# Chunked attention and a maxout layer by seven products: two operands split later, the output products in another order

## The chip, the cores and the metric

The kernel runs on one core of a Trainium2 chip. The metric is the device time of one execution in microseconds (us), given as the median of several runs. Its engines are TensorE (PE in the profile; PEld is its weight load), VectorE (DVE), ScalarE (ACT), GpSimd (POOL) and SyncE (SP), which issues the transfers (DMAs). Each runs its own instructions in the order in which the program lists them and waits where an operand, a bank or a buffer is not ready.

## What is computed

```python
scores = scale * np.matmul(q_c, k_c.transpose(0, 1, 2, 4, 3))    # 576 tokens in chunks of 64
scores = scores - np.max(scores, axis=-1, keepdims=True)
attn = np.exp(scores)
attn = attn / (np.sum(attn, axis=-1, keepdims=True) + 1e-09)
out = np.matmul(attn, v_c)
...
h = np.maximum(np.maximum(x @ w1, x @ w2), x @ w3)               # x: 4608 x 512, w: 512 x 768
return (h @ w_out).astype(np.float32)                            # w_out: 768 x 512
```

Batch 8, 8 heads, head size 64; the attention output of all heads, 4608 tokens of 512 values, goes through a layer that keeps the largest of three products, and then through an output layer. All in float32.

## The kernel before

A float32 matrix product is done as three products of a reduced type: each operand is split into a high part (a cast) and a low part (what the cast lost), and low x high, high x low and high x high are added up in one bank of PSUM. ACT does the casts (`high`), DVE the subtractions (`low`).

The tokens come in tiles of 128. The first 8 tiles (two groups of 4) go through both layers directly, and while they do, the weights are mixed for the rest: the other 28 tiles, in four units of 7, 8, 7 and 6 tiles (`UNITS`), are computed by Strassen's scheme in Winograd's form. It takes seven products of blocks instead of eight; the operands of the products are sums and differences of blocks. Half a unit is 448, 512, 448 or 384 columns wide.

One unit has a hidden phase and an output phase. The hidden phase has nine sets (`sets`: three parts jp of the hidden width, for each of the three weights w). A set is seven products in the order `ORDER` = 1, 6, 5, 2, 7, 3, 4, each of 6 matmuls (L567). Products 2, 7 and 3 add onto the banks of 1, 6 and 5 (`banks_of_product`), once ACT has copied those out (`kept`, L581); five banks are taken in turn. Behind them DVE and POOL form the sums (L584, L587, L591) and the maximum over the three weights (L578). Behind every third set the operands of the output phase are made from the maximum: differences (L609, L621), casts (L614) and lows (L617), called Y. The output phase multiplies the seven Y operands with the mixed output weights, in the order `OUTER`: 18 matmuls a product, in two halves m of 9. Its products are read out by copies (L655, L666) and by DVE's sums (L658), which write the results to one of four output buffers (`ao`) that are stored by SP (L650).

The operands of the next unit's hidden phase, X1 to X7, are made during the output phase of the unit before (`operands`, L500 to L504): differences of blocks of the attention output in `stage` (L489, three by DVE or POOL), casts (L494) and lows (L498). The attention of the next units runs in between, a tile at a time: V, S and T are its products and transposes on PE (L258, L223, L246), `softmax` its steps on the others, and `tiles(u, time)` says when each tile of a unit is due. The output layer's weights are mixed once, by `store_out`: POOL adds (L419, L433), ACT's cast (L438), DVE's low (L441) and stores; `stores_out` plans it into unit 0's first sets. Mixed weights come back from DRAM a piece at a time, issued by SP (L510 for the hidden layer, L518 for the output layer), each into a ring whose previous content has been used.

What sets the order of all this is a list of due times. Every PE step advances a clock `now` by a nominal duration, and what a product leads to is planned at an offset from its end:

```python
    def passed(step):
        nonlocal now
        now += step
        while due and due[0][0] <= now:
            _, _, pe, fn = heapq.heappop(due)
            fn()
```

So the numbers in `operands`, in `after[...]` of `hidden` and in `tiles` and `stores_out` order the instructions on each engine; they are no times of the chip.

Of the kernel before, what the change touches and what calls it, by code (L numbers as in the profile page):

```python
# [31 lines left out]
OUTER = (1, 2, 6, 7, 5, 3, 4)  # L32
SOFTMAX = (("mx", 1.0), ("sub", 1.9), ("exp", 2.8), ("sum", 3.8), ("eps", 4.7), ("rec", 4.9), ("nrm", 5.3))
ON_PE = {"V": 0.6, "S": 0.6, "T": 0.35}
OPERANDS = 0.3
# [28 lines left out]
def chunk_attn_maxout_kernel(  # L64
# [399 lines left out]
    def unit(t0, count, rooms):  # L464
# [35 lines left out]
        def operands():  # L500
            return [(0.0, high(1)), (1.2, low(1)), (2.4, mix(5, b12, b11, nc.vector)), (3.4, high(5)),
                    (3.6, mix(6, b22, source[5], nc.vector)), (4.6, mix(7, b22, b12, nc.gpsimd)), (4.8, high(6)),
                    (5.8, low(6)), (5.9, high(2)), (7.0, low(5)), (8.0, mix(4, b21, source[6], nc.gpsimd)), (8.2, low(2)),
                    (8.3, high(7)), (9.4, low(7)), (9.45, high(3)), (10.6, low(3)), (10.7, high(4)), (11.8, low(4))]  # L504
# [10 lines left out]
        def load_outer(k):  # L515
            def fn():
                outer[k] = next_ring((k + 1) % 2, 6).rearrange("p (j k) x -> p j (k x)", j=3)
                nc.sync.dma_start(out=outer[k].bitcast(F32), in_=outer_w["w"].rearrange(  # L518
                    "p (j i x) -> p j i x", j=3, i=7)[:, :, k])
            return fn  # L520
# [49 lines left out]
        def hidden(n, loads):  # L570
# [3 lines left out]
            def M(k, c):  # L574
                return m()[:, k, c, :half]
# [26 lines left out]
            if w == 2:  # L602
# [17 lines left out]
                def less(eng, out, x, y):  # L620
# [4 lines left out]
                             (1.0, less(nc.gpsimd, t[7], lambda: M(1, 1), lambda: M(0, 1))), (1.6, t6), (1.65, high(2)),  # L625
                             (2.4, low(2)), (2.4, high(6)), (3.1, low(6)),
                             (3.2, less(nc.gpsimd, t[4], lambda: M(1, 0), t[6])), (3.1, high(5)), (3.8, low(5)),
                             (3.8, high(7)), (4.5, low(7)), (4.9, high(3)), (5.6, low(3)), (5.7, high(4)), (6.4, low(4))]
# [52 lines left out]
        return dict(operands=operands, load=load, load_outer=load_outer, hidden=hidden,  # L681
# [151 lines left out]
    def tiles(u, time):  # L833
        if u >= len(units):
            return
        lead = 14.0 if u == 1 else 18.0
# [45 lines left out]

    def stores_out():
        for jp in range(3):
            for at, fn in store_out(jp):
                plan(now + 16.0 + 14.0 * jp + at, 0.0, fn)
# [10 lines left out]
    parts += [("do", change), ("do", lambda: operands(0, OPERANDS)),  # L897
# [3 lines left out]
    for u, (it, t0, count) in enumerate(units):  # L901
# [4 lines left out]
        parts.append(("steps", lambda u=u, it=it: it["project"](loads_within(u))))  # L906
    now = -10.0
# [54 lines left out]
```

## Time and profile before

| | us |
|---|---|
| median of 3 runs | 642.67 (641.45 to 643.28) |
| the profiled execution | 643.57 |
| its span in the trace | 641.8 |

The profile is one execution. "Busy" is the time in which an engine executes; a bracket behind a row is the engine's idle time just before it and what it waited for last. PEclk is the clock that TensorE was granted, as a share of 2.4 GHz. Times are counted from the start of the span.

### The profile page before, as it was taken

To read this page: it belongs to the slowest core of one execution; us is meant where nothing else is said; L and a number is where in the kernel's file an instruction comes from. 1 tells how busy PE (TensorE), PEld (TensorE's weight loads), DVE (VectorE), ACT (ScalarE), POOL (GpSimd) and SP (SyncE) were. 2 spreads that over 40 slices of the span, in tenths; PEclk is the share of its full clock that TensorE was granted. 3 is DMA by queue.
4 is the path that set the end of the run, shared out by engine and by line. 5 is a ranking of instruction groups with operands and counts; after the bars stand their busy time and mean duration, and the time that the engine had idled before them with its cause. 6 is when DMAs were issued, how large, how long until landed. Compare 5 with 4: busy or idle time off the path is not lost.

```text
span 641.8 us, 12694 instructions
## 1 busy us (share of the span) xinstructions
PE 620.8 (97%) x5102; PEld 536.4 (84%) x5102; DVE 445.0 (69%) x684; ACT 269.9 (42%) x483; POOL 277.5 (43%) x235
## 2 busy tenths in 40 slices
PE   7899999999999899998999999989999998999997
PEld 3888878878888789997888888768989888999997
DVE  4889855788856958688368686883477568265762
ACT  4888633444543434362325252622342444232340
POOL 2423577764556824452234343441253434133430
PEclk9999999999999899998999999989999999999999
DMA  8978559666969996586866664759765657877774
GB/s 323 365 291 287 198 182 370 209 223 247 357 198 359 347 323 205 198 275 214 313 215 229 215 225 153 246 183 332 260 198 190 231 166 234 339 260 261 235 225 169
DMA packets 54219, 161.26 MB, mean 251 GB/s; under 512 B 4880, under 2 KB 17168, under 8 KB 49168
## 3 DMA queue, kind: packets, MB, share of 16 engines
q1 hardware_dynamic: 54160, 160.45, 72.2%
q8 instruction: 40, 0.66, 0.4%
q14 instruction: 19, 0.16, 0.1%
HBM read 128.97 MB, written 31.46 MB: 250 GB/s over the span
## 4 chain that ended last, share of the span: by engine, by line
PE 71%; DVE 17%; ACT 5%; issue 4%; POOL 2%; DMA 1%; SPq 0%; ACTq 0%; DVEq 0%; POOLq 0%
PE pm L567 53%; PE pm L173 4%; PE pm L174 4%; PE pm L175 4%; DVE X L498 3%; PE s L258 2%; PE tp L246 2%; DVE most L578 2%; PE s L223 2%; DVE e L233 2%; DVE mx L228 1%; DVE s L384 1%; DVE sm L181 1%; ACT e L237 1%; ACT stage L272 1%
## 5 line engine op out<-in xcount | busy, mean ns | idle before, releaser
L567 PE MATMUL pm<-X,ring 128*128 128x448 f32 (+2 forms) x1512 | 313.3, 367 | 4.4 <-ACT kept L581 3.3
L567 PEld LDWEIGHTS pm<-X,ring 128*128 128x128 f32 x1512 | 278.2, 189 | 32.4 <-ACT kept L581 5.1
L581 ACT COPY kept<-pm 128x448 f32<-128x448 f32 (+2 forms) x108 | 56.8, 532 | 149.9 <-PE pm L567 129.6
L567 PE MATMUL pm<-Y,ring 128*128 128x448 f32 (+2 forms) x504 | 107.7, 373 | 7.7 <-DVE ao L658 7.4
L567 PEld LDWEIGHTS pm<-Y,ring 128*128 128x128 f32 x504 | 94.4, 193 | 19.9 <-DVE ao L658 9.0
L591 POOL TENSOR_TENSOR kept<-kept 128x448 f32<-128x448 f32 (+2 forms) x36 | 43.5, 1209 | 82.5 <-ACT kept L581 82.3
L578 DVE TENSOR_TENSOR most<-pm,most 128x448 f32<-128x448 f32 (+2 forms) x72 | 44.6, 620 | 46.4 <-PE pm L567 45.0
L173 PE MATMUL pm<-xh,wl 128*128 128x512 f32 (+1 forms) x156 | 60.9, 391 | 0.0
L174 PE MATMUL pm<-xl,wh 128*128 128x512 f32 (+1 forms) x156 | 58.4, 375 | 0.3 <-DVE xl L269 0.3
L175 PE MATMUL pm<-xh,wh 128*128 128x512 f32 (+1 forms) x156 | 58.5, 375 | 0.0
L614 ACT CAST Y<-most 128x448 fp32r<-128x448 f32 (+2 forms) x72 | 39.6, 571 | 44.4 <-DVE most L578 44.4
L617 DVE TENSOR_TENSOR Y<-most,Y 128x448 fp32r<-128x448 f32 (+2 forms) x72 | 53.8, 777 | 3.0 <-ACT Y L614 1.6
L190 POOL TENSOR_TENSOR e<-e,sm 128x512 f32<-128x512 f32 x26 | 27.7, 1066 | 60.5 <-DVE sm L187 52.2
L587 POOL TENSOR_TENSOR kept<-kept 128x448 f32<-128x448 f32 (+2 forms) x24 | 30.5, 1269 | 52.0 <-DVE kept L584 43.2
L228 DVE TENSOR_REDUCE mx<-s 128x8 f32<-128x512 f32 x36 | 24.6, 683 | 27.3 <-PE s L223 27.3
L584 DVE TENSOR_TENSOR kept<-pm,kept 128x448 f32<-128x448 f32 (+2 forms) x36 | 22.3, 619 | 25.4 <-PE pm L567 21.8
L233 DVE TENSOR_TENSOR e<-s,mx 128x512 f32<-128x512 f32 x36 | 24.8, 690 | 18.3 <-ACT stage L272 17.6
L237 ACT ACTIVATE e<-e 128x512 f32<-128x512 f32 x36 | 22.7, 632 | 27.7 <-DVE e L233 27.7
L251 ACT COPY xs<-tp 128x512 f32<-128x512 f32 x36 | 21.0, 583 | 31.6 <-PE tp L246 31.6
L173 PEld LDWEIGHTS pm<-xh,wl 128*128 128x128 f32 x156 | 29.4, 188 | 5.4
L175 PEld LDWEIGHTS pm<-xh,wh 128*128 128x128 f32 x156 | 29.4, 188 | 5.4
L584 DVE TENSOR_TENSOR pm<-pm,kept 128x448 f32<-128x448 f32 (+2 forms) x48 | 30.0, 626 | 5.5 <-PE pm L567 4.3
(98 smaller groups left out, 855.6 us busy)
## 6 DMA issues: line engine op xcount, KB each, us to landing
ring<-w SPq DMA_DIRECT2D x36, 1024.0 KB, 5.2
ring<-w SPq DMA_DIRECT2D x36, 768.0 KB, 4.7
ring<-wo SPq DMA_DIRECT2D x28, 768.0 KB, 4.6
buf<-in_qk SPq DMA_DIRECT2D x36, 512.0 KB, 5.9
buf<-in_vb SPq DMA_DIRECT2D x36, 256.0 KB, 5.0
w<-s SPq DMA_DIRECT2D x18, 512.0 KB, 4.4
stage<-in_w SPq DMA_DIRECT2D x7, 512.0 KB, 4.6
out_t<-ao SPq DMA_DIRECT2D x16, 224.0 KB, 4.9
```

Of the source, the lines that this page charges most:

```text
L173: nc.tensor.matmul(out=o, lhsT=al, rhs=bh, start=first, stop=False)
L174: nc.tensor.matmul(out=o, lhsT=ah, rhs=bl, start=False, stop=False)
L175: nc.tensor.matmul(out=o, lhsT=ah, rhs=bh, start=False, stop=last)
L228: nc.vector.tensor_reduce(out=st["mx"].rearrange("p (g c) -> p c g", c=2), in_=st["s"], axis=AX.X, op=ALU.max)
L233: nc.vector.tensor_tensor(out=st["e"].rearrange("p g c k -> p c g k"), in0=st["s"], in1=most.unsqueeze(3).broadcast_to([P, 2, 4, 64]), op= ...
L567: nc.tensor.matmul(out=o[i], lhsT=a, rhs=b, start=new and k == 0, stop=last and k == 2, skip_group_check=i in banks_of_product)
L578: return lambda: nc.vector.tensor_tensor(out=M(k, c), in0=of(), in1=M(k, c), op=most)
L581: return lambda: nc.scalar.copy(out=kept(k), in_=o[i])
L584: return lambda: nc.vector.tensor_tensor(out=out(), in0=o[i], in1=kept(k), op=plus)
L591: (0.95, lambda: nc.gpsimd.tensor_tensor(out=kept(2), in0=kept(2), in1=kept(0), op=plus))],
L614: return lambda: nc.scalar.copy(out=y_room(i, jp)[:, 0, :half], in_=t[i]())
L617: return lambda: nc.vector.tensor_tensor(out=y_room(i, jp)[:, 1, :half], in0=t[i](), in1=y_room(i, jp)[:, 0, :half].bitcast(F32), op=minus)
```

## The change

Four things are changed. First, X3 and X4 leave `operands`; a new list, `last_operands`, makes their casts and lows at the start of the unit that uses them (for unit 0, behind the direct group's projection). Second, in `OUTER` product 4 now stands ahead of product 3, and the transfers of the output weights follow (`load_outer`). Third, the Y operands' casts and lows get other due times: Y5's cast first, Y4 ahead of Y3, and more time between them. Fourth, `store_out` begins 6 nominal us later and its three parts are 17 instead of 14 apart; the tiles of units 2 and 3 begin 2 later.

```diff
-OUTER = (1, 2, 6, 7, 5, 3, 4)
+OUTER = (1, 2, 6, 7, 5, 4, 3)
...
         def operands():
...
-                    (8.3, high(7)), (9.4, low(7)), (9.45, high(3)), (10.6, low(3)), (10.7, high(4)), (11.8, low(4))]
+                    (8.3, high(7)), (9.4, low(7))]
+
+        def last_operands():
+            return [(0.0, high(3)), (1.0, low(3)), (1.1, high(4)), (2.2, low(4))]
...
                 nc.sync.dma_start(out=outer[k].bitcast(F32), in_=outer_w["w"].rearrange(
-                    "p (j i x) -> p j i x", j=3, i=7)[:, :, k])
+                    "p (j i x) -> p j i x", j=3, i=7)[:, :, (0, 1, 2, 3, 4, 6, 5)[k]])
...
                 after[4] += [(0.2, less(nc.vector, t[5], lambda: M(0, 1), lambda: M(0, 0))),
-                             (1.0, less(nc.gpsimd, t[7], lambda: M(1, 1), lambda: M(0, 1))), (1.6, t6), (1.65, high(2)),
-                             (2.4, low(2)), (2.4, high(6)), (3.1, low(6)),
-                             (3.2, less(nc.gpsimd, t[4], lambda: M(1, 0), t[6])), (3.1, high(5)), (3.8, low(5)),
-                             (3.8, high(7)), (4.5, low(7)), (4.9, high(3)), (5.6, low(3)), (5.7, high(4)), (6.4, low(4))]
+                             (1.0, less(nc.gpsimd, t[7], lambda: M(1, 1), lambda: M(0, 1))), (1.0, high(5)), (1.6, t6),
+                             (2.0, high(2)), (2.6, low(2)), (2.6, high(6)),
+                             (3.2, less(nc.gpsimd, t[4], lambda: M(1, 0), t[6])), (3.3, low(5)), (3.4, high(7)),
+                             (4.0, low(6)), (4.7, low(7)), (5.0, high(4)), (5.6, low(4)),
+                             (6.7 if jp == 2 else 3.9, high(3)), (7.4 if jp == 2 else 5.3, low(3))]
...
-        lead = 14.0 if u == 1 else 18.0
+        lead = 14.0 if u == 1 else 20.0
...
+    def last_operands(u, begin=0.1):
+        if u < len(units):
+            for at, fn in units[u][0]["last_operands"]():
+                plan(now + begin + at, 0.0, fn)
+
     def stores_out():
         for jp in range(3):
             for at, fn in store_out(jp):
-                plan(now + 16.0 + 14.0 * jp + at, 0.0, fn)
+                plan(now + 22.0 + 17.0 * jp + at, 0.0, fn)
...
-    parts += [("do", change), ("do", lambda: operands(0, OPERANDS)),
+    parts += [("do", change), ("do", lambda: operands(0, OPERANDS)), ("do", lambda: last_operands(0, 4 * JT * STEP + 0.1)),
...
         parts.append(("steps", lambda u=u, it=it: it["project"](loads_within(u))))
+        parts.append(("do", lambda u=u: last_operands(u + 1)))
```

How this moves instructions is seen at three places; lines are those of each kernel (L658 before is L662 after, L581 is L584, L614 is L617, L650 is L654, L510 is L513).

DVE, from the end of unit 0's output phase into unit 1, before (X3 and X4 are the lows L498; L658 are the sums of products 5, 5, 3, 3, 4, 4; L228 to L187 a softmax):

```order
L498 TENSOR_TENSOR X7_2183<-stage_1530,X7_2183 128x1024
L658 TENSOR_TENSOR ao_3461<-pm_3439,kept_2300 128x448
L498 TENSOR_TENSOR X3_2194<-stage_1530,X3_2194 128x1024
L658 TENSOR_TENSOR ao_3511<-pm_3457,kept_2300 128x448
L498 TENSOR_TENSOR X4_2205<-most_2132,X4_2205 128x1024
L228 TENSOR_REDUCE mx_3520<-s_155 128x2x4
L233 TENSOR_TENSOR e_3527<-s_155,mx_3520 128x2x4x64
L658 TENSOR_TENSOR ao_3539<-pm_3439,kept_2300 128x448
```

and after the change, from the second sum of product 5 (the first stands just ahead of it, behind X7's low):

```order
L662 TENSOR_TENSOR ao_3473<-pm_3456,kept_2297 128x448
L662 TENSOR_TENSOR ao_3527<-pm_3469,kept_2297 128x448
L228 TENSOR_REDUCE mx_3534<-s_155 128x2x4
L233 TENSOR_TENSOR e_3537<-s_155,mx_3534 128x2x4x64
L662 TENSOR_TENSOR ao_3549<-pm_3486,kept_2297 128x448
L181 TENSOR_REDUCE sm_3556<-e_3537 128x8
L184 TENSOR_SCALAR sm_3556<-sm_3556 128x8
L187 RECIPROCAL sm_3556<-sm_3556 128x8
L662 TENSOR_TENSOR ao_3567<-pm_3439,kept_2297 128x448
L662 TENSOR_TENSOR ao_3582<-pm_3456,kept_2297 128x448
L498 TENSOR_TENSOR X3_2265<-stage_1530,X3_2265 128x1024
L498 TENSOR_TENSOR X4_2275<-most_2132,X4_2275 128x1024
```

Both sums of product 5 now follow X7's low directly, then come product 4's and product 3's, and the lows of X3 and X4 stand behind all of them.

SP at the same place, before (`out_t<-ao` are the stores of the sums in their order, `ring<-w0` and `w1` the next unit's weights, `buf` the attention's inputs):

```order
L650 DMA out_t<-ao_3461 128x448
L215 DMA buf_3472<-in_vb 128x512
L510 DMA ring_3514<-w0_1003 128x2048
L211 DMA buf_3516<-in_qk 128x1024
L650 DMA out_t<-ao_3511 128x448
```

and after:

```order
L654 DMA out_t<-ao_3460 128x448
L513 DMA ring_3475<-w0_1003 128x2048
L654 DMA out_t<-ao_3473 128x448
L215 DMA buf_3484<-in_vb 128x512
L211 DMA buf_3529<-in_qk 128x1024
L654 DMA out_t<-ao_3527 128x448
```

The store of product 5's second half now follows the weight load directly; the two inputs come behind it.

ACT around unit 0's fourth set, before (L614 are casts of Y; the L581 with pm_2616, pm_2686 and pm_2704 copy the fourth set's products 1, 6 and 5; L438 is the output weights' cast; L251, L272 and L237 belong to the attention):

```order
L438 CAST so_2575<-c_2472 128x4x256
L614 CAST Y_2592<-most_2132 128x448
L581 COPY kept_2300<-pm_2616 128x448
L614 CAST Y_2674<-most_2132 128x448
L251 COPY xs_2676<-tp_2660 128x512
L272 COPY stage_1530<-s_155 128x2x4x64
L614 CAST Y_2684<-m_2672 128x448
L614 CAST Y_2693<-most_2132 128x448
L237 ACTIVATE e_2690<-e_2690 128x512
L614 CAST Y_2702<-most_2132 128x448
L581 COPY kept_2300<-pm_2686 128x448
L614 CAST Y_2715<-most_2132 128x448
```

and after, from behind Y5's cast (pm_2608, pm_2675 and pm_2691 are those products):

```order
L584 COPY kept_2297<-pm_2608 128x448
L251 COPY xs_2664<-tp_2652 128x512
L272 COPY stage_1530<-s_155 128x2x4x64
L617 CAST Y_2669<-most_2132 128x448
L617 CAST Y_2673<-m_2662 128x448
L617 CAST Y_2686<-most_2132 128x448
L237 ACTIVATE e_2679<-e_2679 128x512
L617 CAST Y_2689<-most_2132 128x448
L584 COPY kept_2297<-pm_2675 128x448
L438 CAST so_2703<-c_2581 128x4x256
L617 CAST Y_2706<-most_2132 128x448
L584 COPY kept_2297<-pm_2691 128x448
```

Y5's cast has come ahead of the copy of product 1; as many casts as before, four, stand between that copy and the copy of product 6; the output weights' cast has moved from ahead of the set to behind the copy of product 6.

## Rows read from the trace of the kernel before

**Rows 1.** Page, part 1: busy us (share of the span) xinstructions.

```profile
PE 620.8 (97%) x5102; PEld 536.4 (84%) x5102; DVE 445.0 (69%) x684; ACT 269.9 (42%) x483; POOL 277.5 (43%) x235
```

**Rows 2.** Waits of PE: engine line waited for: us in total, times, longest us.

```profile
PE pm L567 <- DVE ao L658: 7.4, 4, 2.9
PE pm L567 <- ACT kept L581: 3.3, 3, 2.1
```

**Rows 3.** Timeline of PE: start, us, what, matmuls merged [idle before <-releaser].

```profile
182.52 5.13 PE L567 MATMUL pm<-X,ring 128*128 128x448 f32 x24 [1.08 <-ACT ao L330]
...
204.61 6.47 PE L567 MATMUL pm<-X,ring 128*128 128x448 f32 x30 [0.21 <-ACT kept L581]
...
218.55 7.91 PE L567 MATMUL pm<-X,ring 128*128 128x448 f32 x30 [2.14 <-ACT kept L581]
...
273.16 18.57 PE L567 MATMUL pm<-Y,ring 128*128 128x448 f32 x90
...
296.27 9.20 PE L567 MATMUL pm<-Y,ring 128*128 128x448 f32 x36 [2.86 <-DVE ao L658]
...
406.03 14.65 PE L567 MATMUL pm<-Y,ring 128*128 128x512 f32 x63 [0.26 <-ACT kept L655]
...
422.12 2.32 PE L567 MATMUL pm<-Y,ring 128*128 128x512 f32 x9
427.00 3.92 PE L567 MATMUL pm<-Y,ring 128*128 128x512 f32 x9 [2.56 <-DVE ao L658]
431.25 6.42 PE L567 MATMUL pm<-Y,ring 128*128 128x512 f32 x27 [0.34 <-DVE ao L658]
...
472.41 7.71 PE L567 MATMUL pm<-X,ring 128*128 128x448 f32 x36 [0.98 <-ACT kept L581]
...
543.12 7.55 PE L567 MATMUL pm<-Y,ring 128*128 128x448 f32 x36 [1.65 <-DVE ao L658]
```

**Rows 4.** Windows: stretch, us, each engine's busy time (instructions), PEclk, DMA share, GB/s.

```profile
218.80:222.20 3.40, 3.40 (x11) 3.00 (x11) 3.37 (x8) 1.49 (x4) 2.40 (x3) 0.52 1.06 409
297.30:300.70 3.40, 3.40 (x12) 2.99 (x11) 2.69 (x5) 0.58 (x1) 0.00 (x0) 0.52 0.97 296
...
543.00:546.40 3.40, 3.28 (x16) 3.07 (x17) 2.87 (x5) 0.00 (x0) 0.00 (x0) 1.00 0.75 161
```

**Rows 5.** Timeline of DVE at the end of unit 0's output phase.

```profile
291.42 4.26 DVE L498 TENSOR_TENSOR X<-stage,X 128x1024 fp32r<-128x1024 f32 x2
295.61 0.61 DVE L658 TENSOR_TENSOR ao<-pm,kept 128x448 f32<-128x448 f32 x1
296.14 1.21 DVE L498 TENSOR_TENSOR X<-stage,X 128x1024 fp32r<-128x1024 f32 x1
```

**Rows 6.** Timeline of POOL, in unit 0's third and fourth sets and in its output phase.

```profile
209.41 1.54 POOL L587 TENSOR_TENSOR kept<-kept 128x448 f32<-128x448 f32 x1
...
291.11 2.36 POOL L489 TENSOR_TENSOR most<-stage,most 128x1024 f32<-128x1024 f32 x1 [1.23 <-DVE X L498]
```

**Rows 7.** Timeline of DVE in unit 0's third and fourth sets.

```profile
206.70 1.61 DVE L441 TENSOR_TENSOR so<-c,so 128x1024 fp32r<-128x1024 f32 x1
...
211.06 1.60 DVE L578 TENSOR_TENSOR most<-kept,most 128x448 f32<-128x448 f32 x1
...
213.12 0.62 DVE L584 TENSOR_TENSOR pm<-pm,kept 128x448 f32<-128x448 f32 x1
```

**Rows 8.** Timeline of ACT: the copy that PE waits for at 218.55.

```profile
217.97 0.53 ACT L581 COPY kept<-pm 128x448 f32<-128x448 f32 x1
```

**Rows 9.** SP and DMAs: the load's issue; load, first and second store (us to landing).

```profile
297.15 0.40 SPq L510 DMA_DIRECT2D ring<-w  x1
...
ring<-w SPq DMA_DIRECT2D x1, 1024.0 KB, 5.7
...
out_t<-ao SPq DMA_DIRECT2D x1, 224.0 KB, 1.9
...
out_t<-ao SPq DMA_DIRECT2D x1, 224.0 KB, 7.0
```

More of the change, by code (lines that the diff above doesn't have):

```diff
@@ L679, in project @@
                         yield STEP_H[count], after if jp == 2 else []
-        return dict(operands=operands, load=load, load_outer=load_outer, hidden=hidden,
+        return dict(operands=operands, last_operands=last_operands, load=load, load_outer=load_outer, hidden=hidden,
                     project=project)
```

## Prediction

> **What bounds the kernel now.** I read the busy shares first. TensorE (PE) is busy for 620.8 of 641.8 us, so what a change can still win is PE's idle time, and what follows from it [rows 1]. The list of what PE waited for names it: 7.4 us in four waits for DVE's output sums (L658), 3.3 us in three waits for ACT's copies of a product's bank (L581) [rows 2]. The timeline of PE then says where each wait stands and what comes behind it [rows 3]. In unit 0's output phase PE waits 2.86 us before product 3, because that product adds onto the bank of product 5 and DVE has not yet read product 5 out. Then 36 matmuls take 9.20 us where 90 took 18.57 just ahead, which would make 7.43: 1.77 us more. Unit 1 waits 2.56 us at the same place, and its next 9 matmuls take 3.92 us instead of 2.32 (1.60 more), then 0.34 us. Unit 2 waits 1.65 us and its 36 matmuls take 7.55, as they should. In unit 0's fourth hidden set the wait is 2.14 us, and 30 matmuls take 7.91 instead of 6.47 (1.44 more). The windows show why: behind waits of 2.14 and 2.86 us the granted clock is 0.52 over 3.4 us, mostly the 1.2 GHz level, and behind 1.65 us it stays at 1.00, the 2.4 GHz level [rows 4]. So a wait of over 2 us has cost about 1.6 us extra here, a shorter one nothing. With 1.08 us at unit 0's start, 0.21 in its third set and 0.98 in unit 2's fourth set, these places hold 16.6 us (0.26 us ahead of product 2 in unit 1 is left out, since nothing there changes).
>
> **The change, part by part.** The sum is made against the profiled execution (643.57 us), which lies 0.90 over the median.
>
> *Output order, and X3 and X4 out of the output phase.* Before, DVE ran X7's low, then the sum of product 5, with X lows between the sums [rows 5]. An X low takes 1.21 us alone; the first of the pair of 4.26 us took about 3.05, while POOL mixed X4's source for 2.36 us [rows 5, 6]. Now product 4 stands between 5 and 3, so PE has 18 more matmuls to do before it needs product 5 read out. Unit 0: PE was ready at 296.27 - 2.86 = 293.41 and now runs 18 x 0.206 = 3.7 us of product 4, to 297.1. DVE's sum ended at 296.22. I add 0.5 us, since X1's cast now stands before the last Y cast on ACT and the last Y low on DVE waits for that; no row shows this, the bounds are 0 and one X low (1.21). Done at 296.7, in time by 0.4: I leave 0.2 us and count 2.86 + 1.77 - 0.2 = **-4.4**. Unit 1: ready at 424.44, product 4 lasts 18 x 0.233 = 4.2 (63 such matmuls took 14.65), to 428.6; the sum was there at 427.0 even behind X3's and X4's lows: 2.56 + 1.60 + 0.34 = **-4.5**. Unit 2: ready at 541.47, product 3 at 545.2, the sum at 543.1: **-1.6** with 0.1 left. Product 4's own banks were read out long before (its places in the rotation are those of products 2 and 7), and its weights come at the place in the load order that product 3's had.
>
> *What is late next.* Product 3 is now the last, and its banks are those that the next unit's second and third products take. DVE's sum of product 3's second half writes the output buffer that product 5's second half used (four buffers in turn), so it waits for that store to land. In unit 0 SP now issues the 1 MB weight load ahead of that store. The load took 5.7 us from 297.15; a store with nothing before it landed in 1.9 us, one behind the load in 7.0 [rows 9]. Now: load at 297.1, store at 297.5, landing between 303.4 (0.6 after the load) and 304.5, plus 0.6 for the sum: 304.0 to 305.1. PE ends product 3 at 300.8 and wants the bank two products (12 x 0.233 = 2.8) later, at 303.6. That is 0.4 to 1.5 us, and nothing if the store goes through beside the load. I take **+0.5**, nearest to the load's own row. In unit 1 PE wants it at 435.3 and a store issued at 425.7 has 9 us: 0. Unit 2: 0.1, counted above.
>
> *X3 and X4 at the start of a unit.* Four casts and lows are moved, none added. ACT does the casts during product 3. DVE's lows follow the last sum: 304.0 + 1.21 + 1.21 = 306.4. PE wants X3 at 300.8 + 30 x 0.233 = 307.8 and X4 at 309.2: 0 us, margin 2.6 us; if the cover were gone, each us late is a us of PE. In unit 0 itself they come out of the stretch ahead of unit 0, where the softmax and then ACT's output copy (L330) stood behind them, and the 1.08 us wait ended on that copy [rows 3]: **-1.1**.
>
> *Weight mixing spread out.* POOL's steps for the output weights now begin 6 us later and 17 instead of 14 us apart. DVE's low of them (1.61 us) leaves the third set of unit 0, where DVE was behind: its sum of product 4 ran at 213.12, when POOL had stretched an instruction of 0.6 us to 1.60 [rows 6, 7]. Behind that stand the maximum, the subtraction, ACT's exponential and then ACT's copy of product 6's bank at 217.97 [rows 8], for which PE waits in the fourth set. 1.6 us off the chain, half a us given back to an added cast ahead, leaves a wait of about 1.0; the mixing's cast (L438) now stands between the copies of product 6's and product 5's banks and costs product 3 about 0.6 more. 2.14 + 1.44 - 1.6 = **-2.0**, bounds 0 and -3.6. The first low lands in the second set, ahead of the maximum on which the 0.21 us wait hangs: **+0.4**, bounds 0 and +1.2. The mixed weights are read only in unit 0's eighth set: 0.
>
> *Y casts spread, tiles 2 us later.* In unit 2's third set the attention tile now comes after the fifth product, not the fourth; the copy of product 6's bank still stands behind two casts that wait for DVE: 0.98 to about 0.6, **-0.4**, bounds -1.0 and +1.0. The other sets had no wait and keep their order around the copies: 0.
>
> Sum: -4.4 - 4.5 - 1.6 + 0.5 - 1.1 - 2.0 + 0.4 - 0.4 = **-13.1 us**: 630.5 for such an execution, **629.6** for the median.
>
> **Rivals.**
> *A: the wait moves to the unit boundary.* DVE's sum of product 3 is held by the store as above, but by 7.0 us of landing in units 0 and 2: 1.5 us and, in unit 2 (store at 544.3, sum done at 551.9, bank wanted at 551.0), 0.9, less the 0.6 counted, +1.8; with one of the two grown past 2 us the clock falls too, +3.4: 631.4 to **633.0**. For it: the 7.0 us row. Against: that store had two input loads more ahead of it. The Trainium skill (DMA: Bandwidth & Descriptors, "Queues, rings and completion order") has each DMA engine take descriptors in ring order while later ones may complete earlier; by its first half the store follows the load, as in that row, by its second this wait could be nothing.
> *B: POOL's steps cost as much where they now stand.* Moving 18 POOL instructions only changes which DVE instructions they stretch; the fourth set keeps its 3.6 us and the second set's loss doubles: +2.4, **632.0**. For it: both long DVE instructions ran beside POOL [rows 5 to 7]. The Trainium skill (SBUF, "Who interferes with whom") states that a DVE instruction with two SBUF inputs and a POOL instruction that reads SBUF exclude each other for the whole instruction, which those rows bear out. Against: DVE idles between sets elsewhere, and a stretched instruction there costs nothing.
> *C: unit 0's sum of product 5 is still late.* The margin is 0.4 us. One more stretched X low (3.05 for 1.21) makes a wait of 1.4 us there, and by over 2 us the clock falls too: +1.2 to +3.4, **632**. So the reorder would have done little in this unit.
> *D, slower: X4's low is late in all four units.* With the landing of A (305.1) and both lows stretched to 3.05 us, X4 is ready at 311.2, 2.0 us after PE wants it, and the clock falls: 4 x 3.6 = +14.4, **644.0**. It decides where X4's low ends about 2 us late; below that a unit loses under 2 us and the change still wins. Against: POOL has no step as long as that mixing there, and unit 1 has no such store.
>
> **How the numbers follow.** Forecast 0.60, A 0.15, B 0.10, C 0.10, D 0.03, something that leaves the time within the bound 0.02. About 0.3% (1.9 us) is what a measurement of this kernel can tell from no change. Low end: every wait of the list gone, 642.67 - 16.6, **626.0**. High end: A and B together are 635.4; a further wait of 1 us somewhere among the reordered tiles makes **636.0**. Forecast, A, B and C all lie beyond 1.9 us: faster 0.95, same 0.02, slower 0.03.
>
> **What would show it.** In the changed profile L658 should be nearly gone from what PE waited for, and no clock of 0.5 should stand in an output phase: that settles 10.5 us. ACT's L330 should be gone at unit 0's start. A (bank): PE waits for a DVE sum at the third product of a unit. B: PE waits for ACT's bank copy in unit 0's second or fourth set, with the clock down. D: PE waits for L498 at the sixth or seventh product of a unit. If PE's idle time falls by 8 us or more and the time doesn't, I have misread what PE's idle time is worth; if L658's wait stays, the reorder did not free DVE.

## The result, and the profile after

The changed kernel takes **633.0 us** (median of 4 runs, 631.67 to 633.18) against 642.84 (641.45 to 643.28) for the kernel before on the same chip: a ratio of 0.9846, 95% interval 0.9826 to 0.9866, or 9.8 us less. Forecast were 629.6 us, 13.1 less; the time lies inside the range (626.0 to 636.0), on its upper half. The profiled execution takes 633.14 us with a span of 631.4, 10.4 less than the profiled execution before.

The page of the changed kernel, part 1, answers to [rows 1]; the waits of PE, below it, to [rows 2]. From L504 on a line of the changed kernel has the number of the old one plus 3, from L650 on plus 4.

```profile
PE 616.8 (98%) x5101; PEld 533.6 (85%) x5102; DVE 446.9 (71%) x684; ACT 271.7 (43%) x483; POOL 281.2 (45%) x235
```

```profile
PE pm L570 <- ACT kept L584: 4.1, 5, 1.8
...
PE pm L570 <- DVE ao L662: 0.6, 1, 0.6
PE pm L570 <- ACT kept L659: 0.5, 2, 0.3
```

DVE's output sums held PE for 7.4 us in four waits; now for 0.6 in one. ACT's bank copies held it for 3.3 us in three waits; now for 4.1 in five. PE's timeline shows where these are, and that the output phases of units 0 to 2 (295.37, 420.64, 513.90) run on where [rows 3] had waits of 2.86, 2.56 and 1.65 us.

```profile
203.92 6.36 PE L570 MATMUL pm<-X,ring 128*128 128x448 f32 x30 [0.61 <-ACT kept L584]
...
217.44 8.03 PE L570 MATMUL pm<-X,ring 128*128 128x448 f32 x30 [1.84 <-ACT kept L584]
...
247.58 0.87 PE L570 MATMUL pm<-X,ring 128*128 128x448 f32 x3 [0.33 <-ACT kept L584]
...
295.37 5.18 PE L570 MATMUL pm<-Y,ring 128*128 128x448 f32 x24
...
338.62 2.49 PE L570 MATMUL pm<-X,ring 128*128 128x512 f32 x9 [0.27 <-ACT kept L584]
...
420.64 8.44 PE L570 MATMUL pm<-Y,ring 128*128 128x512 f32 x36
...
513.90 25.86 PE L570 MATMUL pm<-Y,ring 128*128 128x448 f32 x126
...
542.47 63.71 PE L570 MATMUL pm<-X,ring 128*128 128x384 f32 x366 [0.61 <-DVE ao L662]
```

Each set begins with its first matmul, so start less start gives what it took, in both traces. This table is worked out so; it adds a wait and what follows from it (slow matmuls, refilling) together.

| stretch | before | after | change | forecast |
|---|---|---|---|---|
| unit 0, first set | 11.54 | 10.19 | -1.35 | -1.1 |
| unit 0, third set | 9.18 | 9.49 | +0.31 | +0.4 |
| unit 0, fourth set | 14.19 | 13.97 | **-0.21** | -2.0 |
| unit 0, seventh set | 10.20 | 10.79 | **+0.59** | 0 |
| unit 0, output phase | 32.15 | 27.45 | -4.70 | -4.4 |
| unit 1, first set | 11.28 | 11.23 | -0.05 | +0.5 |
| unit 1, fourth set | 11.23 | 12.30 | **+1.07** | 0 |
| unit 1, output phase | 35.96 | 31.49 | -4.48 | -4.5 |
| unit 2, fourth set | 9.92 | 9.80 | -0.13 | -0.4 |
| unit 2, output phase | 27.60 | 25.70 | -1.91 | -1.6 |
| unit 3, first set | 7.31 | 8.19 | **+0.88** | 0 |

The sets and phases not shown add up to -0.7 us and none of them moved by more than 0.4; what stands ahead of unit 0 took 0.27 more. That first part, 178.84 us before and 179.11 after, took 177.4 to 179.1 us in the traces of the runs below, also where nothing in it was changed, so spans can differ by 1.7 us for that alone, and what a part of the change is worth is read from the stretches.

What was forecast of the output phases came true, 11.1 us where 10.5 were expected; the gain was lost in the four bold places, by 4.3 us in all against their forecast. ACT's and DVE's timelines show the first of them, unit 0's fourth set.

```profile
211.19 0.57 ACT L617 CAST Y<-most 128x448 fp32r<-128x448 f32 x1 [4.51 <-DVE most L624]
211.66 0.53 ACT L584 COPY kept<-pm 128x448 f32<-128x448 f32 x1
212.09 0.59 ACT L251 COPY xs<-tp 128x512 f32<-128x512 f32 x1
213.53 0.59 ACT L272 COPY stage<-s 128x512 f32<-128x512 f32 x1 [0.85 <-DVE mx L228]
214.01 0.57 ACT L617 CAST Y<-most 128x448 fp32r<-128x448 f32 x1
...
215.88 0.63 ACT L237 ACTIVATE e<-e 128x512 f32<-128x512 f32 x1 [0.36 <-DVE e L233]
216.41 0.55 ACT L617 CAST Y<-most 128x448 fp32r<-128x448 f32 x1
216.87 0.52 ACT L584 COPY kept<-pm 128x448 f32<-128x448 f32 x1
```

```profile
212.28 0.61 DVE L612 TENSOR_TENSOR m<-most 128x448 f32<-128x448 f32 x1
212.81 0.69 DVE L228 TENSOR_REDUCE mx<-s 128x8 f32<-128x512 f32 x1
214.61 0.63 DVE L620 TENSOR_TENSOR Y<-most,Y 128x448 fp32r<-128x448 f32 x1 [1.12 <-ACT Y L617]
215.16 0.68 DVE L233 TENSOR_TENSOR e<-s,mx 128x512 f32<-128x512 f32 x1
```

PE waits for the copy at 216.87, that of product 6's bank. The mixing's low (L441) has left the third set as foreseen, and DVE's maximum (L228) starts 3.91 us after the set's first matmul (208.90); in the kernel before it was 5.17 (214.85 - 209.68), so it is 1.26 us earlier. The copy starts 7.97 us after that matmul, in the kernel before 8.29 (217.97 [rows 8] less 209.68): 0.32 earlier. Between the two 0.94 us are given back. Y2's cast has moved: at 2.0 in the list, not 1.65, it stands behind the tile's stage copy (L272), and that waits for the maximum. Y2's low, ahead of the tile's subtraction (L233), waits for the cast: DVE idles 1.12 us with the subtraction, the exponential and the bank copy behind it.

### The profile page after: what moved, and what is told of

Read it like the earlier page. It is cut to its first block, busy times and chain, and to the rows that moved or that the text cites. A ratio compares the mean times of both kernels' runs of the same rounds, so it can differ in the third digit from the quotient of the medians.

```text
span 631.4 us, 12685 instructions
## 1 busy us (share of the span) xinstructions
PE 616.8 (98%) x5101; PEld 533.6 (85%) x5102; DVE 446.9 (71%) x684; ACT 271.7 (43%) x483; POOL 281.2 (45%) x235
## 4 chain that ended last, share of the span: by engine, by line
PE 80%; DVE 11%; ACT 4%; issue 2%; POOL 1%; DMA 1%; DVEq 0%; POOLq 0%; ACTq 0%
PE pm L570 55%; PE pm L173 6%; PE pm L174 6%; PE pm L175 6%; PE s L258 3%; PE tp L246 2%; PE s L223 2%; DVE most L581 1%; DVE e L233 1%; DMA out_t<-ao 1%; DVE sm L181 1%; DVE mx L228 1%; PE pm L737 1%; DVE X L498 1%; DVE s L384 1%
## 5 line engine op out<-in xcount | busy, mean ns | idle before, releaser
L584 ACT COPY kept<-pm 128x448 f32<-128x448 f32 (+2 forms) x108 | 57.1, 532 | 115.1 <-PE pm L570 98.1
L570 PE MATMUL pm<-Y,ring 128*128 128x448 f32 (+2 forms) x504 | 103.8, 365 | 0.5 <-ACT kept L659 0.5
L570 PEld LDWEIGHTS pm<-Y,ring 128*128 128x128 f32 x504 | 92.2, 188 | 10.7 <-ACT kept L659 2.1
L581 DVE TENSOR_TENSOR most<-pm,most 128x448 f32<-128x448 f32 (+2 forms) x72 | 44.7, 621 | 45.9 <-PE pm L570 44.6
L594 POOL TENSOR_TENSOR kept<-kept 128x448 f32<-128x448 f32 (+2 forms) x36 | 46.2, 1283 | 62.7 <-ACT kept L584 62.6
L617 ACT CAST Y<-most 128x448 fp32r<-128x448 f32 (+2 forms) x72 | 40.4, 568 | 65.7 <-DVE most L624 44.9
L620 DVE TENSOR_TENSOR Y<-most,Y 128x448 fp32r<-128x448 f32 (+2 forms) x72 | 51.5, 744 | 5.7 <-ACT Y L617 4.5
L590 POOL TENSOR_TENSOR kept<-kept 128x448 f32<-128x448 f32 (+2 forms) x24 | 30.6, 1277 | 49.3 <-DVE kept L587 44.7
L251 ACT COPY xs<-tp 128x512 f32<-128x512 f32 x36 | 21.0, 584 | 49.9 <-PE tp L246 49.9
L228 DVE TENSOR_REDUCE mx<-s 128x8 f32<-128x512 f32 x36 | 24.6, 683 | 23.2 <-PE s L223 23.2
L233 DVE TENSOR_TENSOR e<-s,mx 128x512 f32<-128x512 f32 x36 | 24.8, 690 | 18.0 <-ACT stage L272 17.7
L237 ACT ACTIVATE e<-e 128x512 f32<-128x512 f32 x36 | 22.8, 633 | 28.3 <-DVE e L233 28.3
```

The lines of the kernel that those rows point to most:

```text
L228: nc.vector.tensor_reduce(out=st["mx"].rearrange("p (g c) -> p c g", c=2), in_=st["s"], axis=AX.X, op=ALU.max)
L233: nc.vector.tensor_tensor(out=st["e"].rearrange("p g c k -> p c g k"), in0=st["s"], in1=most.unsqueeze(3).broadcast_to([P, 2, 4, 64]), op= ...
L570: nc.tensor.matmul(out=o[i], lhsT=a, rhs=b, start=new and k == 0, stop=last and k == 2, skip_group_check=i in banks_of_product)
L581: return lambda: nc.vector.tensor_tensor(out=M(k, c), in0=of(), in1=M(k, c), op=most)
L584: return lambda: nc.scalar.copy(out=kept(k), in_=o[i])
L594: (0.95, lambda: nc.gpsimd.tensor_tensor(out=kept(2), in0=kept(2), in1=kept(0), op=plus))],
```

## Experiments

Each run is given by its median and its ratio to the kernel before on the same chip (641.25 us beside runs 1 to 4, 642.3 beside runs 5 to 8, 643.26 beside runs 9 to 11 and 642.47 beside run 12), since these medians differ by more than a part of the change, on one chip too (runs 1 to 4 and 5 to 8). What a single place took is read from the traces as in the table.

**1. The old times of the Y casts, in the changed kernel.**

```diff
-(1.0, high(5)), (1.6, t6), (2.0, high(2)), (2.6, low(2)), (2.6, high(6)), ...
+(1.6, t6), (1.65, high(2)), (2.4, low(2)), (2.4, high(6)), ..., (3.1, high(5)), ...
```

> The changed kernel with the due times of the Y casts and lows as before (products 3 and 4 exchanged in the list, since they exchanged places); all else as changed (633.0 us). My theory: Y5's cast, due at 1.0, stands on ACT ahead of the copy of product 1's bank and waits there for DVE's subtraction L624, so that copy is late in unit 0's seventh and unit 1's fourth set (0.59 and 1.07 us); and in unit 0's fourth set Y2's cast stands behind the tile's stage copy L272, so DVE idles 1.12 us ahead of the tile's subtraction and the copy of product 6's bank gets back all that the mixing's low had cost. With the old times the two losses go (-1.7), the copy of product 6's bank comes about 1.1 us earlier, the wait of 1.84 us falls to about 0.7 and the clock holds (-2.7): 628.6 us; if the clock falls all the same, 630.2. Rival, POOL: the fourth set is late because POOL's mixing stretches DVE's instructions there; then 1.84 us stay and only the two losses go, 631.3. Rival, output phase: the spread casts are what lets the output phases run without waits; then L662 or L659 holds PE there again and the time rises to about 636.

In this run and in run 4, Y3's low in the last unit is listed behind POOL's sum that overwrites what it reads, so product 3 of that unit gets a partly wrong operand; the same instructions run, and both runs are read for their times alone.

Measured: 628.76 us, 0.9801 (0.9769 to 0.9833). The fourth set takes 12.00 us (-1.97), the seventh 10.20 (-0.59). Now Y2's cast is ahead of L272 and nothing idles in between; PE's wait is 0.91 and 0.36 us in place of 1.84, and the clock holds. So in this set the casts' new times took back most of what the mixing had gained (run 2), as ACT's timeline of this run shows:

```profile
211.28 0.57 ACT L617 CAST Y<-most 128x448 fp32r<-128x448 f32 x1 [1.50 <-DVE most L581]
211.76 0.58 ACT L251 COPY xs<-tp 128x512 f32<-128x512 f32 x1
212.42 0.59 ACT L272 COPY stage<-s 128x512 f32<-128x512 f32 x1
...
214.82 0.53 ACT L584 COPY kept<-pm 128x448 f32<-128x448 f32 x1
```

The stage copy now waits for nothing, and the bank copy starts 7.03 us after the set's first matmul (207.79), not 7.97. The seventh set's loss is of another kind: in the changed kernel Y5's cast stands ahead of the copy of product 1's bank, and the two rows from ACT's timeline show it waiting there for DVE's subtraction, with the copy behind it; PE waits for that copy at 247.58.

```profile
246.53 0.57 ACT L617 CAST Y<-most 128x448 fp32r<-128x448 f32 x1 [4.82 <-DVE most L624]
247.00 0.53 ACT L584 COPY kept<-pm 128x448 f32<-128x448 f32 x1
```

But unit 1's fourth set stays at 12.29: that part of my theory fell, the loss there is not Y5's cast. Unit 1's output phase takes 0.6 us less in this run, which was not foreseen.

**2. The old mixing, in the changed kernel.**

```diff
-plan(now + 22.0 + 17.0 * jp + at, 0.0, fn)
+plan(now + 16.0 + 14.0 * jp + at, 0.0, fn)
```

> The changed kernel with the output weights' mixing at its old times (16 us, then every 14 us, in place of 22 and 17). My theory: DVE's low of 1.2 to 1.6 us is back in unit 0's third set, so the chain of maximum, subtraction, exponential and bank copy in the fourth set is 1.2 us later, the wait of 1.84 us becomes about 3: 634.3 us; the second set's wait of 0.61 us goes at the same time (-0.5), so 633.8 in all. Rival, POOL costs the same wherever its steps stand: 633.0 within 0.3. Second rival, the chain is set by the Y casts that wait on ACT and not by the low: 632.5, the fourth set unchanged and the second set's wait gone.

Measured: 633.62 us, 0.9875 (0.9843 to 0.9908). The fourth set takes 16.38 us, 2.41 more, the third 0.30 less. The wait became 3.07 us, as expected; its consequence was larger, since the clock stayed at 0.50 for 6.7 us, the 1.2 GHz level, twice as long as behind 1.84 us. Moving the mixing was worth 2.1 us at these two places. The span moved by 0.6 only, since the part ahead of unit 0 was 1.4 us shorter in this trace. The two rows are PE's timeline and the window behind the wait.

```profile
216.98 7.35 PE L570 MATMUL pm<-X,ring 128*128 128x448 f32 x21 [3.07 <-ACT kept L584]
```

```profile
216.40:223.10 6.70, 6.12 (x16) 5.47 (x17) 5.67 (x10) 2.05 (x6) 5.16 (x6) 0.50 0.81 316
```

What came back on DVE is the mixing's low (L441). POOL's steps stretch DVE's instructions with either timing: two of them between the low and the maximum take 1.60 and 0.61 us in this run, as in the kernel before, and 0.93 and 1.15 in the changed kernel, with other steps of the mixing beside them; that is 2.21 us against 2.08. DVE's timeline in this run, then in the changed kernel:

```profile
204.20 1.61 DVE L441 TENSOR_TENSOR so<-c,so 128x1024 fp32r<-128x1024 f32 x1
...
208.56 1.60 DVE L581 TENSOR_TENSOR most<-kept,most 128x448 f32<-128x448 f32 x1
210.09 0.61 DVE L624 TENSOR_TENSOR most<-most 128x448 f32<-128x448 f32 x1
```

```profile
209.16 0.93 DVE L581 TENSOR_TENSOR most<-kept,most 128x448 f32<-128x448 f32 x1
210.01 1.15 DVE L624 TENSOR_TENSOR most<-most 128x448 f32<-128x448 f32 x1
```

**3. Five output buffers, in the changed kernel.**

```diff
-tag=f"ao{len(outputs) % 4}"
+tag=f"ao{len(outputs) % 5}"
```

> The changed kernel with five output buffers in turn in place of four. My theory: at the start of the fourth unit PE waits 0.61 us (0.88 in all with the refilling behind it) for DVE's sum of product 3's second half, which waits for the store of product 5's second half, issued 0.44 us behind a 1 MB weight load and landed 6.15 us later. With five buffers that sum takes the buffer of product 5's first half, whose store was issued ahead of the load and landed in 2.05 us: the wait goes, 632.2 us. Rival: what the sum waits for is not the buffer but something else of that time (the bank, POOL): no change, 633.0.

Measured: 630.98 us, 0.9832 (0.9801 to 0.9864); unit 3's first set takes 7.31 us (-0.88), no other set or phase changes by over 0.12. First DVE's last sum of unit 2 in the changed kernel (timeline of DVE), which ends a wait on a store; then SP's timeline of the same kernel, with that store's issue (the first of the two at 535.52) behind a 1 MB load's; then the load and that store, and the store ahead of the load, with their us from issue to landing; then the sum in this run (timeline of DVE), which runs as soon as PE is done.

```profile
541.79 0.62 DVE L662 TENSOR_TENSOR ao<-pm,kept 128x448 f32<-128x448 f32 x1 [3.19 <-DMA out_t<-ao]
```

```profile
534.65 0.34 SPq L654 DMA_DIRECT2D out_t<-ao  x1
535.08 0.38 SPq L513 DMA_DIRECT2D ring<-w  x1
535.52 0.92 SPq L654 DMA_DIRECT2D out_t<-ao  x2
```

```profile
ring<-w SPq DMA_DIRECT2D x1, 1024.0 KB, 6.0
out_t<-ao SPq DMA_DIRECT2D x1, 224.0 KB, 6.1
...
out_t<-ao SPq DMA_DIRECT2D x1, 224.0 KB, 2.1
```

```profile
537.95 0.62 DVE L662 TENSOR_TENSOR ao<-pm,kept 128x448 f32<-128x448 f32 x1 [1.20 <-PE pm L570]
```

So the wait is for the store of that buffer. That the store lands late because of the load ahead of it rests on these landings; no run was made that issues it ahead of the load.

**4. The exchange of products 3 and 4 alone**, on the kernel before (`OUTER`, the weights' places and the two casts' times).

> The kernel before (642.8 us) with nothing but the exchange of products 4 and 3 in the output phase (with the weights' places and the Y casts' two times exchanged with it); X3 and X4 are still split inside the output phase, the other times are the old ones. My theory: the exchange alone gives all of the output phases' gain, since DVE's sum of product 5 was done at 296.2, 427.0 and 543.1 us even with the X lows between, and PE now wants it at 297.1, 428.6 and 545.2: -2.86 - 1.77 - 2.56 - 1.60 - 0.34 - 1.65 = -10.8, 632.0 us, with up to 0.9 lost again at the start of the fourth unit: 632.9. Rival: the X lows between the sums make product 4's and 3's sums late in turn, at least one wait of over 2 us stays with its clock (3 to 4.5 us): 635 to 637.

Measured: 632.4 us (631.0 to 635.66), 0.987 (0.9821 to 0.992). The output phases take 4.52, 4.04 and 1.50 us less, 10.1 of the 10.8 expected; the next unit's first set pays 0.60 for a bank (the place foreseen at unit 0's end), and a wait of 0.74 us for one of DVE's output sums stays in unit 1's output phase. The exchange carries the gain there. Outside these phases unit 0's fourth set took 1.45 us less, which no edit of this run explains; it is taken up in the last section.

**5. A lead of 18 for the tiles, in the changed kernel.**

```diff
-lead = 14.0 if u == 1 else 20.0
+lead = 14.0 if u == 1 else 18.0
```

> The changed kernel (633.0 us) with the attention tiles of the third and fourth unit 18 us behind the start of the output phase, as before, in place of 20. My theory: unit 1's fourth set lost 1.07 us to the lead, not to the Y casts (the old cast times left its 12.3 us as they were): its tile moved behind product 7, so the tile's subtraction and sum on DVE stand nearer to the Y lows, and the copies of three banks come late. With 18 us that set takes 11.23 again: 631.9 us. Rival: the set's loss comes from the Y casts' spread and the lead together, or from the exchanged products; it keeps 12.3 us: 633.0.

Measured: 631.25 us, 0.9825 (0.9798 to 0.9851). Unit 1's fourth set takes 11.23 us again (-1.07), so the lead made the loss. Its first set loses 0.57 in this run, 0.3 of it PE waiting for an X low at the unit's sixth product, which is the sign that the prediction gave for rival D, and its seventh 0.23.

**6. X3 and X4 at the start of the unit alone**, on the kernel before.

> The kernel before (642.8 us) with nothing but X3's and X4's casts and lows moved to the start of the unit that uses them. My theory: it leaves unit 0's and unit 2's output phases nearly as they are, since the sum of product 5's first half, for which PE waits, stands ahead of X3's low on DVE there (2.9 and 1.7 us of waits stay, with the clock's 1.8 us in unit 0), and helps unit 1, whose sum stands behind both lows (2.1 of 2.56 us go and the clock holds: -3.7); unit 0's start gains 1.2: 637.9 us. Rival, DVE's load is what matters, not the order: all three phases gain two lows' time, waits of 2.86, 2.56 and 1.65 fall by 2.4, 2.1 and 1.65 with the clock's share: -4.2 - 4.1 - 1.65 - 1.2, 631.7 us.

Measured: 639.15 us, 0.9949 (0.9931 to 0.9966). Unit 0's start gains 1.35, its output phase nothing, unit 1's 2.22, unit 2's nothing; unit 0's fourth set loses 0.66. My theory holds for the order of size and the rival does not: the order on DVE counts, not its load. In unit 1 I was too high, since the tile's maximum, subtraction and sum moved up into the lows' place and the next sum of product 5 waited behind them; PE waits 0.59 and 1.65 us there.

**7. Three things mended at once**: Y2 and Y5 as in run 1, five buffers, lead 18.

> The changed kernel with three things mended at once: Y2's and Y5's casts at their old due times (1.65 and 3.1) with the rest of the spread kept (Y3's at 4.8), five output buffers, and a lead of 18 us. My theory adds up what the single runs showed: unit 0's fourth set 12.0 us for 13.97 (-1.97), its seventh -0.59, unit 1's fourth -1.07, unit 3's first -0.88: -4.5 from 633.0, 628.5 us. Rival: the gains overlap, since work that is no longer late in one place is late in the next; less than 3 us in all, 630 or more.

Measured: 628.97 us, 0.9787 (0.9757 to 0.9817). The four bold stretches take 12.46, 10.20, 11.23 and 7.31 us, 4.05 less in all of the 4.5 expected, so they nearly add up. The fourth set is 0.5 over run 1's: two Y casts and not one now stand ahead of the copy of product 5's bank, and PE's wait for it is 0.82 us, in run 1 0.36.

**8. The stage copy ahead of the maximum**, and Y7's cast behind the copy of product 6's bank, on top of run 7.

```diff
-plan(at + 1.0, 0.0, lambda n=n: steps(n)["x"]())
+plan(at + 0.95, 0.0, lambda n=n: steps(n)["x"]())
```

> As the run with three things mended, and two more: Y7's cast due after the copy of product 6's bank in the next set, and the tile's stage copy L272 put ahead of DVE's maximum L228, for which it was seen to wait. My theory: unit 0's fourth set loses another 0.5 to 1.3 us of wait (copy of product 6's bank 0.5 earlier, casts behind L272 up to 0.8 earlier), the third set its 0.3: 627.5 us. Rival: the two read one bank, so the maximum now waits for the copy instead, subtraction and exponential come 0.6 us later, and the set gains nothing: 628.5.

Measured: 633.21 us, 0.9859 (0.9823 to 0.9894): slower than run 7. The rival was right and too mild. The maximum now waits for the copy and everything behind it is late, in unit 2's fourth set too (10.49 us, 9.96 in run 7). Y7's new place is not the reason: run 10 has it too, and gains in the fourth set. The two rows are from the timelines of ACT and of DVE in this run.

```profile
212.72 0.59 ACT L272 COPY stage<-s 128x512 f32<-128x512 f32 x1
```

```profile
213.35 0.69 DVE L228 TENSOR_REDUCE mx<-s 128x8 f32<-128x512 f32 x1 [1.07 <-ACT stage L272]
```

**9. The exchange and X3/X4 together, with the old times**, on the kernel before (three due times of Y4 and Y3 are 0.1 to 0.3 earlier than in run 1, so that Y3's low stands ahead of the sum that overwrites what it reads).

> The kernel before (642.8 us) with the exchange of products 4 and 3 and with X3's and X4's split at the start of the unit that uses them, and none of the changed times (Y casts in the old list, mixing at 16 and 14 us, lead 18). My theory: these two carry nearly all of the change's gain. Unit 0's start -1.35, the three output phases -4.6, -4.4 and -1.8, the fourth set unchanged, and one bank wait of 0.6 to 0.9 us at the start of the fourth unit: 631.4 us, so that the three changed times together brought about nothing or a loss (633.0). Rival: without the spread casts and the moved mixing the output phases keep waits, or the fourth set's wait grows as it did when X3 and X4 were moved alone (+0.7): 633 to 636, and the times were needed.

Measured: 630.05 us, 0.9802 (0.9778 to 0.9826). The output phases take 4.77, 5.08 and 1.50 us less, unit 0's start 1.35; the fourth set stays (14.35), no bank wait appears at a unit's start. So these two parts carry more than the whole change did. The changed times together cost 1.9 us by the stretches (2.8 by the ratios, whose intervals just touch): the mixing gives 2.1, the casts take 2.0 and 0.6, the lead 1.07, and unit 3's store wait, 0.88, holds PE only with them (in run 9 DVE's last sum of unit 2 waits for the store too, 2.2 us, but ends in time). The single prices, taken in other surroundings, add up to more than the 1.9.

**10 to 12. Bank copies ahead of casts.** On top of run 7, run 10 puts Y7, Y4 and Y3 behind the copies in unit 0's fourth set and the mixing 2 us later; run 11 also puts Y2 and Y6 behind the copy of product 6's bank in units 1 to 3; run 12, for the second third (jp = 1) alone, gives Y4 and Y3 their times of run 7 again and puts Y2 and Y6 behind that copy in unit 0 too. The edit of run 10, cut at "...":

```diff
-(3.8, high(7)), ..., (5.0, high(4)), ..., (6.7 if jp == 2 else 4.8, high(3)), ...
+(4.3, high(7)), ..., (5.5, high(4)), ..., (6.7 if jp == 2 else 5.4, high(3)), ...
...
-plan(now + 22.0 + 17.0 * jp + at, 0.0, fn)
+plan(now + 24.0 + 17.0 * jp + at, 0.0, fn)
```

> As the run with three things mended (627.0 us of span, 0.9787 of before), and the Y casts that stood ahead of bank copies in unit 0's fourth set put behind them: Y7's behind the copy of product 6's bank, Y4's behind the copy of product 5's, and the mixing's cast behind both (mixing 2 us later); the tile's copy L272 and the maximum stay as they were. My theory: that set waits twice, 0.91 us before product 7 and 0.82 before product 3, with 2.3 us more than a set without a wait; one cast of 0.5 leaves the first wait (0.4 left), a cast and the mixing's 1.06 leave the second (0 left): 12.46 becomes 10.8, so -1.6, ratio 0.976. Rival: the chain through DVE's subtraction and the exponential sets the first wait, and the moved low of the mixing meets another set's maximum: -0.5 or less, or a loss.

> As the run before it in this list, and in units 1 to 3 the casts of Y2 and Y6 due after the copy of product 6's bank. My theory: in unit 2's fourth set PE waits 0.98 us for that copy, which stands behind Y2's cast, and that cast waits 2.4 us for DVE; the copy goes ahead, the wait goes (-0.9), and -0.2 in unit 1's seventh set: ratio 0.9745. Rival: Y2's low and POOL's subtraction of Y4 are then late and the copies behind them with them: no gain, or one bank copy further on is late instead.

> As the run with the copies first in the late units too (0.9775 of before, span 625.3 us), with the second set of Y operands of unit 0 to 3 treated apart: there Y3's and Y4's casts keep their places ahead of the tile's stage copy (4.8 and 5.0), and Y2 and Y6 go behind the copy of product 6's bank in unit 0 as well. My theory: in unit 0's eighth set PE waited 0.89 us for ACT's L599, which stood behind Y3's and Y4's casts, and those behind the tile's copy L272, which waited 2.2 us for DVE's maximum; the set took 11.62 us, 10.2 without, and the seventh 0.3 more than without. Both go: -1.7, ratio 0.975, span 623.6. Rival: the casts only move the wait to the copy of product 5's bank in the seventh set: no gain over 0.5.

Measured: run 10 629.76 us, 0.9797 (0.9773 to 0.9821); the fourth set falls to 11.45, but the seventh and eighth lose 1.74 us: their casts, put later, land behind the tile's stage copy, with ACT's copy of product 2 (L599) behind them. Run 11 628.16 us, 0.9775 (0.9752 to 0.9798); unit 2's fourth set falls by 0.78 of the 0.9 expected, and the 0.2 in unit 1's seventh set did not come. Run 12 **627.10 us**, 0.9757 (0.9738 to 0.9777), the lowest, and clear of the changed kernel's interval, but not of run 7's or run 11's; unit 0's seventh and eighth sets gain 1.16 of the 1.7 expected. PE's timeline of run 12 shows what is left of the fourth set's wait:

```profile
215.84 6.58 PE L570 MATMUL pm<-X,ring 128*128 128x448 f32 x30 [0.82 <-ACT kept L584]
```

## Why the prediction was right, and where not

*The output phases: right.* Product 4 between 5 and 3 gave DVE the time, and the forecast for each phase was off by 0.3 us at most. Runs 4, 6 and 9 show that the exchange does it, that X3 and X4 alone gain 2.2 us in unit 1 and nothing in units 0 and 2, and that together they also clear run 4's leftover wait in unit 1. In unit 0 it was close, as rival C feared: the first sum of product 5, first of the three in this row of DVE's timeline, ends at 296.6, and PE begins product 3 (the 7th matmul of its row at 295.37) at 296.67.

```profile
295.97 1.67 DVE L662 TENSOR_TENSOR ao<-pm,kept 128x448 f32<-128x448 f32 x3
```

*Unit 0's start and its third set: right*, -1.35 for -1.1 and +0.31 for +0.4; run 6 gives the first from X3 and X4 alone.

*The fourth set: the step failed.* "1.6 us off the chain, half a us given back to an added cast ahead" had the mixing right (run 2: 2.4 us of this set) and left out that the list of casts puts Y2's behind the stage copy. Of the 1.26 us by which the maximum came earlier, 0.94 were given back. With all the casts' old times the set takes 1.97 us less (run 1), with Y2's and Y5's alone put back 1.51 (run 7). Rival B said that the set would keep its loss, and it did. Of B's reason one half holds: POOL's steps still stretch DVE there, by nearly as much. But moving the mixing was worth 2.4 us all the same, with its low gone from this chain (run 2). The POOL row that the prediction sets beside the stretched maximum (209.41, 1.54 us, [rows 6]) had ended before that maximum began (211.06, [rows 7]); what ran beside it was a step of the mixing, from POOL's timeline of the kernel before:

```profile
210.91 1.26 POOL L419 TENSOR_TENSOR f<-woh,wol 128x512 f32<-128x512 f32 x1
```

*"The other sets had no wait and keep their order around the copies: 0": failed.* In unit 0's seventh set Y5's cast passed the copy of product 1's bank and held it up, which cost the set 0.59 us (run 1, and run 7 with Y2's and Y5's casts alone put back). In unit 1's fourth set the tiles' lead, which I costed only in unit 2, took 1.07 (run 5); through which of the tile's steps was not tried. In unit 2's fourth set it brought 0.13 of the 0.4 us forecast.

*The bank at a unit's end: the mechanism of rival A, in unit 2 where I had counted 0.1.* Its price there, 0.9 us, was right: 0.88 measured, and run 3 shows that the wait is for the store. At unit 0's end the store held the last sum too, for 1.23 us, but the +0.5 did not come. The step that failed is "its banks are those that the next unit's second and third products take": PE starts unit 1's third product, the 13th matmul of the second row, at 303.1 without a wait, ahead of that sum, so it is not on that sum's bank. The rows are DVE's and PE's timelines of the changed kernel.

```profile
303.23 0.62 DVE L662 TENSOR_TENSOR ao<-pm,kept 128x448 f32<-128x448 f32 x1 [1.23 <-DMA out_t<-ao]
```

```profile
300.38 9.02 PE L570 MATMUL pm<-X,ring 128*128 128x512 f32 x39
```

That the time is the 633.0 of rival A is chance: A came to it by late banks at two units' ends and a fall of the clock behind one of them, and of that only the 0.88 us was there.

*"A wait of over 2 us has cost about 1.6 us extra, a shorter one nothing": failed.* Behind 1.84 us the clock was 0.50, the 1.2 GHz level, for the 3.4 us shown by this window of the changed kernel, and 30 matmuls took 8.03 us where they take 6.36 (the rows at 217.44 and 203.92): 1.7 us of the missing gain. The step also took what followed a wait in one execution as what always follows it (see the last section).

```profile
218.20:221.60 3.40, 3.40 (x10) 2.69 (x9) 3.37 (x7) 1.47 (x4) 1.91 (x2) 0.50 0.61 230
```

## What to carry to other kernels

When a list of due times orders several engines, a time changed for one reason reorders every queue that it passes: count, for each engine and each set, what now stands ahead of the instruction that PE waits for, and what that one itself waits for. A gain on one chain (the mixing's low) can be given back on another to the same copy (a cast behind a tile's copy); test parts alone before they are kept together. Copies that free a bank belong ahead of casts that wait for another engine, as long as the casts put off do not land ahead of the next such copy (run 10).

## What was not expected of the hardware

*The clock does not go by the length of a wait alone.* At the same copy of the same set, 2.28 us of idle PE left the granted clock at 1.00 in run 4 and 2.27 us were followed by 0.50 in run 9; 1.84 us were followed by 0.50 in the changed kernel. PE's timeline at the wait and the window behind it, run 4 and then run 9:

```profile
217.24 6.35 PE L567 MATMUL pm<-X,ring 128*128 128x448 f32 x30 [2.28 <-ACT kept L581]
...
217.50:220.90 3.40, 3.40 (x18) 3.15 (x18) 3.37 (x8) 1.49 (x4) 2.41 (x3) 1.00 1.05 410
```

```profile
216.87 5.33 PE L570 MATMUL pm<-X,ring 128*128 128x448 f32 x17 [2.27 <-ACT kept L584]
...
218.10:221.40 3.30, 3.30 (x11) 2.81 (x10) 3.27 (x8) 0.52 (x2) 2.29 (x3) 0.50 1.03 414
```

18 matmuls in 3.40 us against 11 in 3.30. Run 4's fourth set therefore took 12.74 us and run 9's 14.35, with the same wait. Executions of one and the same program differ in this too: of the nine of the kernel before that were timed beside runs 9 to 11, the five with a mean granted clock of 0.992 took 643.3 to 644.3 us, the one with 0.999 took 640.8. The profiled execution from which the prediction read what a wait costs has 0.992. What decides it was not tried. The Trainium skill (TensorE: Matmul & The Clock Gate, "Part 1: The HAM clock gate") has the chip's observation run on its own, not started by the kernel. If so, the same idle time can fall differently; these two windows agree with that.

*Two readers of one bank go one after the other.* ACT's stage copy (L272) and DVE's maximum (L228) read different halves of the same PSUM banks; in the changed kernel the copy starts 0.03 us after the maximum ends, in run 8 the maximum 0.04 after the copy, and the profile names the other engine as what ended the wait. The Trainium skill (PSUM — Partial Sum Buffer, "PSUM bank collisions raise a hardware error") has software order two engines on one bank, reads against reads too; these rows agree.
